# Chunked attention and an ELU feed-forward layer in fp32: unit 0's weights loaded ahead of v, nine element-wise operations moved to GpSimd, a new order of the head

## The chip, the cores and the metric

One core of a Trainium2 chip runs the whole program. The metric is the time of one execution in microseconds, as the device reports it; the number given is the median of three runs. Lower is better.

## The reference

```python
def _attn_ref(q, k, v):                 # (8, 8, 576, 64) each, float32
    # chunks of 64 tokens: q_c, k_c, v_c
    scores = scale * np.matmul(q_c, k_c.transpose(0, 1, 2, 4, 3))
    scores = scores - np.max(scores, axis=-1, keepdims=True)
    attn = np.exp(scores)
    attn = attn / (np.sum(attn, axis=-1, keepdims=True) + 1e-09)
    return np.matmul(attn, v_c).reshape(B, H, S, D)

def _moe_ref(x, w_in, w_out):           # x (4608, 512), w_in (512, 2048), w_out (2048, 512)
    h = x @ w_in
    g = np.where(h > 0.0, h, alpha * (np.exp(np.minimum(h, 0.0)) - 1.0))
    return g @ w_out
# x is the attention's output with the heads put side by side: (batch * seq, heads * head_dim)
```

## The kernel before

**Tiles and blocks.** The 4608 tokens are cut into 36 tiles of 128 tokens (two chunks of 64), four tiles to a block of 512, nine blocks. A tile's attention for all eight heads gives 128 rows of x; a block's four tiles give x of 512 tokens, on which the feed-forward layer works: 16 products H0 to H15 (a slice of 128 hidden units each, `hidden`, 12 matmuls of 128x512), each followed by the elu and by a second product O0 to O15 that adds to four accumulators (`second`, 12 matmuls).

**Words of two parts.** The layer's products run in a reduced fp32 format with high and low words: x = xhi + xlo, w = hi + lo, g = ghi + glo, and each product is the sum of three (high by high, high by low, low by high). So every weight slice has to be prepared once. A unit u is the input weights of slice u and the output weights of slice u - 1 (unit 0 has input weights alone). `load_unit` loads it from memory (L118, L125) into one of three buffers; the weights lie there in another format, and `prepare_units` (ScalarE, L139 and L144) and `merge_units` (VectorE: a clamp L161, two merges L168 and L172; then ScalarE casts the high words, L179) make fp32 of them. `subtract_next` makes the low words: lo = w - hi (L185, one instruction for wi_lo, one for wo_lo).

**The head.** `early_attention` makes the first tiles. Its steps: TensorE transposes q and k (L270), ScalarE copies them (L277), TensorE makes the scores (L248), VectorE takes the largest and subtracts it (L283, L299), ScalarE takes the exponential (L303), VectorE sums, adds, inverts and multiplies (L305 to L308, the last being the product of the probabilities with 1 / z), TensorE turns the probabilities (L315), ScalarE copies them (L322), TensorE multiplies by v (L256), and the result goes to xhi on ScalarE (L425) and xlo on VectorE (L426), or is kept for a later block (L420). For tiles 2, 4 and 5 (`BY_HEAD`) the exponential runs as eight instructions with their sums (L293), and VectorE has no sum to make.

**The order.** The engines' orders are written by hand, as strings of items that the program reads one after another; an item issues one step, and each engine runs its instructions in the order in which they were issued. `START` holds the four tiles of block 0 and first units: `q0`, `k0`, `v0` are loads of a tile on SP's queue, `u0` the load of a unit, a digit the next step of that tile, `r` the next step of ScalarE on a unit, `d` the next of VectorE, `s` a subtraction. `FIRST_BLOCK` holds block 0's layer with the attention of tiles 4 to 7 and the other units: `H` a first product, `e` the next of four steps of an elu (relu and exponential on ScalarE, L468 and L469; elu step on VectorE, L471; ghi on ScalarE, L476; glo on VectorE, L479), after whose last the second product waits to be issued, `P` that second product, `L4` the loads of tile 4. SP's queue issues the loads in the order of the items as well. GpSimd does nothing here until it forms sums of weights from about 120 us on (`combine`, L510). Later blocks (`SECOND_BLOCK` and on) follow with other strings.

Of the kernel before, what the change touches and what calls it, by code (L numbers as in the profile page):

```python
# [10 lines left out]
F32 = mybir.dt.float32  # L11
# [9 lines left out]
def kernel(  # L21
# [19 lines left out]
    nc = tc.nc  # L41
# [138 lines left out]
                merged.append((parts[i], w))  # L180
            yield

    def subtract_next():
        (hi, lo), w = merged.pop(0)
        nc.vector.tensor_tensor(out=lo, in0=w, in1=hi.bitcast(F32), op=ALU.subtract)  # L185

    preparation = prepare_units()
    merged = []
# [72 lines left out]
    def first_halves(pair_of_banks):  # L261
        return pair_of_banks[:, :, :NK * C].rearrange("p i (h t) -> p i h t", h=NK)

    def early_attention(tt: int, q_sb, k_sb, get_v, kT, at, a_pool, get_banks, put, by_head: bool):


        both = get_banks()
        for i, src in enumerate((q_sb, k_sb)):
            for hp in range(NK):
                nc.tensor.transpose(  # L270
                    out=both[:, i, hp * P:(hp + 1) * P], in_=src[:, 2 * hp:2 * hp + 2, :],
                    identity=ident,
                )
# [12 lines left out]
        z = sm.tile([P, 2, NK, 1], F32, name="z")
        if by_head:

            nc.vector.tensor_scalar_mul(mx, mx, -SCALE)
            yield  # L290
            for j in range(2):
                for h in range(NK):
                    nc.scalar.activation(  # L293
                        out=a_heads[:, j, h, :], in_=scores[:, j, h, :], func=AF.Exp, scale=SCALE,
                        bias=mx[:, j, h, :], accum_out=z[:, j, h, :],
                    )
            yield
        else:
            nc.vector.tensor_tensor(  # L299
                out=a_heads, in0=scores, in1=mx.broadcast_to([P, 2, NK, C]), op=ALU.subtract  # L300
            )
            yield
            nc.scalar.activation(out=a, in_=a, func=AF.Exp, scale=SCALE)  # L303
            yield
            nc.vector.tensor_reduce(out=z, in_=a_heads, axis=AX.X, op=ALU.add)  # L305
        nc.vector.tensor_scalar_add(z, z, 1e-9)
        nc.vector.reciprocal(z, z)
        nc.vector.tensor_tensor(  # L308
            out=a_heads, in0=a_heads, in1=z.broadcast_to([P, 2, NK, C]), op=ALU.mult
        )  # L310
# [129 lines left out]
    def hidden(f: int):  # L440
        hi, lo = w_in_slices(f)
        h = ps_h.tile([P, TB], F32, name="h")
        if f:
            for kt in range(NK):
                three(h, hi[:, kt, :], lo[:, kt, :], xhi[:, kt, :], xlo[:, kt, :],
                      kt == 0, kt == NK - 1)
        else:
            terms = [(w, xhi, kt) for w in (hi, lo) for kt in range(NK)]
            terms += [(hi, xlo, kt) for kt in range(NK)]
            for i, (w, x, kt) in enumerate(terms):  # L450
                nc.tensor.matmul(h, lhsT=w[:, kt, :], rhs=x[:, kt, :], start=i == 0,  # L451
                                 stop=i == len(terms) - 1)
        return h
# [564 lines left out]
    def warm(n: int):  # L1018
# [5 lines left out]

    BY_HEAD = (2, 4, 5)
    START = (
        "q0 k0 q1 k1 w13 v0 0 1 0 q2 0 k2 q3 0 k3 1 1 v1 0 2 v2 1 3 0 2 2 v3 1 2 3 u0 3 1 2 u1 0 "
        "r r 1 3 1 0 3 2 2 d u2 d 1 0 r d 3 3 2 s 2 0 r d 1 d 3 r 2 3 3"  # L1030
    )
    FIRST_BLOCK = (
# [7 lines left out]
    )  # L1040
    SECOND_BLOCK = (
# [83 lines left out]
    w0 = ctx.enter_context(tc.tile_pool(name="w0", bufs=1))  # L1125
    weights.append((*w_in_tiles(w0), *w_out_tiles(w0)))
    with (
        tc.tile_pool(name="start", bufs=NTT) as start,
        tc.tile_pool(name="ps_start", bufs=NTT, space=bass.MemoryType.PSUM) as ps_start,
    ):  # L1130
# [6 lines left out]
        def start_step(item: str):  # L1137
            tt = int(item)
            if tt not in tiles:
                tiles[tt] = early_attention(  # L1140
                    tt, *[loaded[kind, tt] for kind in "qk"], lambda: loaded["v", tt],
                    start.tile([P, NK, P], F32, name="kT"), start, start,
                    lambda: start_banks() if tt else warmed[0],
                    split_first_x, tt in BY_HEAD)
            next(tiles[tt])

        for item in START.split():
# [5 lines left out]
            elif kind in "qkv":  # L1153
                loaded[kind, int(n)] = load_heads(
                    {"q": q, "k": k, "v": v}[kind], f"{kind}_sb", int(n) * P, start)
            elif kind == "r":
                next(preparation)
            elif kind == "d":
                next(merging)
            elif kind == "s":  # L1160
                subtract_next()
            else:
                start_step(item)

# [48 lines left out]
    for item in FIRST_BLOCK.split():  # L1213
# [12 lines left out]
            next(early_tiles[item])  # L1226
        elif item == "d":
            next(merging)
        elif item == "s":
            subtract_next()  # L1230
        elif item == "r":
            next(preparation)
        elif item[0] == "u":
# [711 lines left out]
```

## Time and profile before

| | |
|---|---|
| time, median of 3 runs | 825.24 us (823.83 to 828.67) |
| the profiled execution's own time | 825.15 us |
| its span | 823.4 us |
| TensorE busy | 804.4 us (98% of the span) |
| VectorE busy | 613.1 us (74%) |
| ScalarE busy | 523.5 us (64%) |
| GpSimd busy | 171.1 us (21%) |
| granted clock of TensorE over the span | 0.999 of full speed |

The span is the time from the first to the last instruction of the program in the profile; the execution's time has 1.75 us around it. Busy shares are means over stages that differ: the head, in which the first tiles pass from engine to engine, and the long rest, in which matmuls follow each other. PE in the profile is TensorE, PEld its weight loads, DVE VectorE, ACT ScalarE, POOL GpSimd; L315 is line 315 of the kernel before.

### The profile page before, as it was taken

The numbers are of one execution on the slowest core, as the hardware profiler recorded it, in microseconds if no ns is written. First come the engines' busy times: TensorE is split into PE (matmuls) and PEld (weight loads), VectorE is DVE, ScalarE is ACT, GpSimd is POOL, SyncE is SP. The second block draws the span as 40 slices with busy tenths as digits, with TensorE's granted clock in tenths as the row PEclk, the third lists the DMA queues.
The fourth block names the chain that finished last, engine by engine and source line by source line (L and its number), as shares of the span: only waits on it lengthen the run. The fifth ranks groups of instructions, "written<-read, shape, count | busy, mean of one in ns | idle before, by whom it ended". The sixth has DMA issues, their size and how long they took to land.

```text
span 823.4 us, 15851 instructions
## 1 busy us (share of the span) xinstructions
PE 804.4 (98%) x5853; PEld 655.6 (80%) x5853; DVE 613.1 (74%) x914; ACT 523.5 (64%) x990; POOL 171.1 (21%) x149
## 2 busy tenths in 40 slices
PE   6799999999999999999999999999999999999997
PEld 5688878888778878878888888778788888888885
DVE  4999997666776659767656867868889956557964
ACT  5999885544554546766666445888867737776451
POOL 0000014264525531443111254000020100000100
PEclk9999999999999999999999999999999999999999
DMA  9976994889778887689986789999876585566755
GB/s 234 272 212 209 270 328 130 244 243 267 219 215 231 231 269 205 202 241 281 283 235 188 218 246 299 286 322 287 249 204 206 195 269 193 193 196 190 226 186 149
DMA packets 183229, 191.90 MB, mean 233 GB/s; under 512 B 84720, under 2 KB 151792, under 8 KB 183152
## 3 DMA queue, kind: packets, MB, share of 16 engines
q1 hardware_dynamic: 182512, 188.80, 77.2%
q0 software_dynamic: 640, 2.10, 0.6%
q8 instruction: 46, 0.75, 0.4%
q14 instruction: 31, 0.25, 0.1%
HBM read 144.18 MB, written 42.99 MB: 227 GB/s over the span
## 4 chain that ended last, share of the span: by engine, by line
PE 83%; DMA 8%; SPq 3%; ACT 2%; DVE 2%; issue 1%; DVEq 0%; ACTq 0%
PE o L434 43%; PE h L434 34%; DMA ring<-a_dram 3%; PE ps_a L248 2%; PE ps_a L256 2%; SPq L206 2%; PE h L451 1%; DMA st<-in_moe_w_out_dram 1%; DMA kept<-in_k_dram 1%; DMA a_dram<-wi_lo 1%; DMA kept<-in_q_dram 1%; DMA a_dram<-wi_hi 1%; DMA v_sb<-in_v_dram 1%; PE ps_a L315 1%; DMA ring<-w_dram 1%
## 5 line engine op out<-in xcount | busy, mean ns | idle before, releaser
L434 PE MATMUL o<-wo_hi,ghi 128*128 128x512 f32 x272 | 107.6, 396 | 0.0
L434 PE MATMUL o<-wo_hi,glo 128*128 128x512 f32 x272 | 106.1, 390 | 0.3 <-DVE glo L479 0.3
L434 PE MATMUL o<-wo_lo,ghi 128*128 128x512 f32 x272 | 106.0, 390 | 0.0
L434 PE MATMUL h<-xhi,wi_hi 128*128 128x512 f32 x228 | 84.0, 397 | 0.1
L434 PE MATMUL h<-xlo,wi_hi 128*128 128x512 f32 x228 | 82.3, 390 | 0.0
L434 PE MATMUL h<-xhi,wi_lo 128*128 128x512 f32 x180 | 70.3, 390 | 0.0
L434 PEld LDWEIGHTS o<-wo_hi,glo 128*128 128x128 f32 x272 | 51.1, 188 | 11.7 <-DVE glo L479 0.7
L434 PEld LDWEIGHTS o<-wo_hi,ghi 128*128 128x128 f32 x272 | 51.0, 188 | 11.1
L434 PEld LDWEIGHTS o<-wo_lo,ghi 128*128 128x128 f32 x272 | 51.1, 188 | 10.2
L510 POOL TENSOR_TENSOR kept<-wi_hi,wi_lo 128x512 f32<-128x512 f32 x16 | 21.7, 1376 | 158.8 <-DVE xf L172 118.2
L471 DVE SCALAR_TENSOR_TENSOR e<-e,h 128x512 f32<-128x512 f32 x48 | 32.8, 684 | 25.2 <-ACT e L469 24.8
L434 PE MATMUL o<-split,ring 128*128 128x512 f32 x216 | 51.0, 390 | 0.0
L434 PEld LDWEIGHTS h<-xhi,wi_hi 128*128 128x128 f32 x228 | 42.6, 188 | 9.8 <-ACT kept L785 0.8
L434 PEld LDWEIGHTS h<-xlo,wi_hi 128*128 128x128 f32 x228 | 42.8, 188 | 8.5
L434 PEld LDWEIGHTS o<-split,ring 128*128 128x128 f32 x216 | 40.5, 188 | 8.4
L393 ACT COPY unturned<-turned 128x512 f32<-128x512 f32 x28 | 17.4, 621 | 46.0 <-DVE turned L388 37.9
L468 ACT ACTIVATE e<-h 128x512 f32<-128x512 f32 x48 | 28.6, 596 | 25.0 <-PE h L434 22.5
L476 ACT CAST ghi<-e 128x512 fp32r<-128x512 f32 x48 | 29.8, 621 | 19.8 <-DVE e L471 19.6
L746 POOL TENSOR_TENSOR glo<-e,ghi 128x512 fp32r<-128x512 f32 x16 | 20.7, 1296 | 96.9 <-ACT ghi L744 96.9
L434 PE MATMUL h<-split,ring 128*128 128x512 f32 x168 | 40.3, 391 | 0.0
L1492 ACT ACTIVATE e<-e 128x512 f32<-128x512 f32 x64 | 39.5, 630 | 1.0
L434 PEld LDWEIGHTS h<-xhi,wi_lo 128*128 128x128 f32 x180 | 33.8, 188 | 7.5 <-DVE wi_lo L185 0.4
(225 smaller groups left out, 2011.3 us busy)
## 6 DMA issues: line engine op xcount, KB each, us to landing
ring<-a_dram SPq DMA_DIRECT2D x56, 512.0 KB, 5.3
ring<-w_dram SPq DMA_DIRECT2D x56, 512.0 KB, 4.3
wi_hi<-a_dram SPq DMA_DIRECT2D x56, 256.0 KB, 5.3
kept<-in_q_dram SPq DMA_DIRECT2D x100, 128.0 KB, 3.8
kept<-in_k_dram SPq DMA_DIRECT2D x100, 128.0 KB, 4.0
wo_lo<-lo_dram SPq DMA_DIRECT2D x20, 512.0 KB, 5.8
v_sb<-in_v_dram SPq DMA_DIRECT2D x32, 256.0 KB, 5.4
st<-in_moe_w_in_dram SPq DMA_DIRECT2D x16, 512.0 KB, 4.9
```

The costliest lines, as they stand in the source:

```text
L206: nc.sync.dma_start(out=dst[p0:p0 + n], in_=src[b, :, s0:s0 + n, :].rearrange("h s d -> s h d"))
L248: nc.tensor.matmul(scores[halves[c], j, hp, :], lhsT=qT[halves[j], hp, halves[c]], rhs=kT[halves[j], hp, halves[c]], start=True, stop=True,)
L256: nc.tensor.matmul(x_ps[halves[j], c, hp, :], lhsT=v_sb[halves[c], 2 * hp + j, :], rhs=aT[halves[c], :, j * NK + hp], start=True, stop=True,)
L315: nc.tensor.matmul(turned_ps[half, h, :], lhsT=a[half, h, :], rhs=ident[half, half], start=True, stop=True,)
L393: nc.scalar.copy(out=unturned, in_=turned)
L434: nc.tensor.matmul(ps, lhsT=a, rhs=b, start=start, stop=stop, skip_group_check=onto)
L468: nc.scalar.activation(out=e, in_=h, func=AF.Relu, scale=-1.0)
L471: nc.vector.scalar_tensor_tensor(out=e, in0=e, scalar=-1.0, in1=h, op0=ALU.add, op1=ALU.max)
L476: nc.scalar.copy(out=ghi, in_=e)
L510: nc.gpsimd.tensor_tensor(out=out, in0=a, in1=b, op=op)
L746: engine.tensor_tensor(out=lo, in0=e, in1=hi.bitcast(F32), op=ALU.subtract)
L1492: nc.scalar.activation(out=units[u], in_=units[u], func=AF.Exp, scale=-1.0)
```

## The change

Four parts. Lines below L183 move by one, those of the layer by one or two, so that L308 before is L309 now, L471 is L472.

1. On SP's queue the first unit's load stands ahead of the v of the first tiles, the second unit's between v0 and v1; q3 and k3 change places. Tile 4's loads stand ahead of unit 3's.
2. `early_attention` gets an argument: for tiles 1 and 2 the product of the probabilities with 1 / z runs on GpSimd. The block of the head schedules GpSimd by hand as well.
3. A second kind of subtraction item, `S`, runs on GpSimd; seven of `FIRST_BLOCK`'s are of that kind.
4. `START` and the first third of `FIRST_BLOCK` have a new order. For H1 and H2 the twelve matmuls come, as for H0, as three groups of four, now with the low words of w last.

```diff
-    def subtract_next():
+    def subtract_next(engine=nc.vector):
         (hi, lo), w = merged.pop(0)
-        nc.vector.tensor_tensor(out=lo, in0=w, in1=hi.bitcast(F32), op=ALU.subtract)
+        engine.tensor_tensor(out=lo, in0=w, in1=hi.bitcast(F32), op=ALU.subtract)
...
-        nc.vector.tensor_tensor(
+        (nc.gpsimd if normal_on_pool else nc.vector).tensor_tensor(
             out=a_heads, in0=a_heads, in1=z.broadcast_to([P, 2, NK, C]), op=ALU.mult
         )
...
-        if f:
+        if f > 2:
             for kt in range(NK):
                 three(h, hi[:, kt, :], lo[:, kt, :], xhi[:, kt, :], xlo[:, kt, :],
                       kt == 0, kt == NK - 1)
         else:
-            terms = [(w, xhi, kt) for w in (hi, lo) for kt in range(NK)]
-            terms += [(hi, xlo, kt) for kt in range(NK)]
+            terms = [(hi, x, kt) for x in (xhi, xlo) for kt in range(NK)]
+            terms += [(lo, xhi, kt) for kt in range(NK)]
...
+    ENGINE_OF = {"s": nc.vector, "S": nc.gpsimd}
...
-        "q0 k0 q1 k1 w13 v0 0 1 0 q2 0 k2 q3 0 k3 1 1 v1 0 2 v2 1 3 0 2 2 v3 1 2 3 u0 3 1 2 u1 0 "
+        "q0 k0 q1 k1 w13 0 1 q2 0 0 k2 0 k3 q3 u0 v0 u1 v1 v2 v3 1 2 1 1 0 0 2 1 2 r r 1 d 3 2 "
...
-        "H r u3 r d L4 d e s 4 d 4 e e s r d e u4 H d s 4 e s r P e 4 d e e H 4 e d 4 L5 e s u5 d P "
+        "H d L4 r e d s 4 r u3 r 4 d e d e u4 S r d e H d 4 s s e P e 4 r e e H d P 4 e d e s "
...
+        tc.manual_schedule(engines={mybir.EngineType.Pool}),
...
-                    split_first_x, tt in BY_HEAD)
+                    split_first_x, tt in BY_HEAD, tt in (1, 2))
...
-            elif kind == "s":
-                subtract_next()
+            elif kind in "sS":
+                subtract_next(ENGINE_OF[kind])
```

**The loads.** SP's queue from tile 1's k on, before. `st` is the buffer of a unit's weights, `q_sb`, `k_sb`, `v_sb` those of a tile.

```order
L206 DMA k_sb<-in_k_dram 128x8x64
L206 DMA v_sb<-in_v_dram 128x8x64
L206 DMA q_sb<-in_q_dram 128x8x64
L206 DMA k_sb<-in_k_dram 128x8x64
L206 DMA q_sb<-in_q_dram 128x8x64
L206 DMA k_sb<-in_k_dram 128x8x64
L206 DMA v_sb<-in_v_dram 128x8x64 x3
L118 DMA st<-in_moe_w_in_dram 128x4x256 x2
L125 DMA st<-in_moe_w_out_dram 128x1024
```

And now, from the load behind tile 1's k on:

```order
L206 DMA q_sb<-in_q_dram 128x8x64
L206 DMA k_sb<-in_k_dram 128x8x64 x2
L206 DMA q_sb<-in_q_dram 128x8x64
L118 DMA st<-in_moe_w_in_dram 128x4x256
L206 DMA v_sb<-in_v_dram 128x8x64
L118 DMA st<-in_moe_w_in_dram 128x4x256
L125 DMA st<-in_moe_w_out_dram 128x1024
L206 DMA v_sb<-in_v_dram 128x8x64 x3
```

Unit 0's weights were the thirteenth load and are the ninth; unit 1's stood behind them and now stand between v0 and v1.

**ScalarE between the last tile of block 0 and the scores of tile 4, before.** `xhi` are the casts that H0 needs, L468 and L469 the relu and exponential of H0, L139 and L144 the two steps on a unit, L179 the casts of a unit's high words.

```order
L425 CAST xhi<-ps_a 128x2x4x64
L322 COPY qT<-ps_a 128x512
L139 ACTIVATE st<-st 128x1024
L425 CAST xhi<-ps_a 128x2x4x64 x2
L144 ACTIVATE st<-st 128x1024
L139 ACTIVATE st<-st 128x1024
L179 CAST wi_hi<-xf 128x512
L179 CAST wo_hi<-xf 128x4x4x32
L468 ACTIVATE e<-h 128x512
L469 ACTIVATE e<-e 128x512
L277 COPY qT<-ps_a 128x512
```

And now (L469 and L470 are the relu and the exponential of H0):

```order
L426 CAST xhi<-ps_a 128x2x4x64 x3
L139 ACTIVATE st<-st 128x1024
L144 ACTIVATE st<-st 128x1024
L139 ACTIVATE st<-st 128x1024
L469 ACTIVATE e<-h 128x512
L470 ACTIVATE e<-e 128x512
L179 CAST wi_hi<-xf 128x512
L179 CAST wo_hi<-xf 128x4x4x32
L144 ACTIVATE st<-st 128x1024
L139 ACTIVATE st<-st 128x1024
L278 COPY qT<-ps_a 128x512
```

The three casts to xhi stand together. Unit 1's first step, which stood ahead of them, stands behind them; the casts of unit 1, unit 2's second step and unit 3's first, which stood ahead of H0's relu, stand behind its exponential.

**VectorE ahead of H3, before.** The three rows on z and a are tile 4's; L471 is the elu step of H2.

```order
L172 SCALAR_TENSOR_TENSOR xf<-st,xf 128x1024
L306 TENSOR_SCALAR z<-z 128x8
L307 RECIPROCAL z<-z 128x8
L308 TENSOR_TENSOR a<-a,z 128x512
L471 SCALAR_TENSOR_TENSOR e<-e,h 128x512
L185 TENSOR_TENSOR wi_lo<-xf,wi_hi 128x512
```

And now, from the load behind tile 1's k on:

```order
L172 SCALAR_TENSOR_TENSOR xf<-st,xf 128x1024
L472 SCALAR_TENSOR_TENSOR e<-e,h 128x512
L185 TENSOR_TENSOR wi_lo<-xf,wi_hi 128x512
L307 TENSOR_SCALAR z<-z 128x8
L308 RECIPROCAL z<-z 128x8
L309 TENSOR_TENSOR a<-a,z 128x512
```

Tile 4's three steps moved from ahead of the elu step of H2 to behind it and behind a subtraction.

## Rows read from the trace of the kernel before

**Rows 1.** The line of the page on the engines' busy time, its share of the span and the number of instructions.

```profile
PE 804.4 (98%) x5853; PEld 655.6 (80%) x5853; DVE 613.1 (74%) x914; ACT 523.5 (64%) x990; POOL 171.1 (21%) x149
```

**Rows 2.** The table of stretches: the stretch in us, its length, then for TensorE (PE), its weight loads, VectorE, ScalarE and GpSimd the busy us (and instructions), granted clock of TensorE, share of the DMA engines, GB/s.

```profile
0.00:29.00 29.00, 17.75 (x430) 15.32 (x431) 16.94 (x33) 18.71 (x43) 0.70 (x6) 1.00 0.92 251
29.00:200.00 171.00, 171.00 (x1303) 138.47 (x1304) 143.28 (x196) 123.02 (x216) 38.38 (x37) 1.00 0.80 240
```

**Rows 3.** The list of TensorE's waits over the whole run: who waited, for whom, us in total, times, longest.

```profile
PE ps_a L315 <- DVE a L308: 3.6, 3, 1.6
PE ps_a L270 <- DMA k_sb<-in_k_dram: 2.2, 3, 1.6
```

**Rows 4.** Timeline of TensorE: start in us, us, line, operation, out<-in, shapes, count, and in brackets the idle time before and what ended it. The transposes of k of tile 2 and of q and k of tile 3 (L270), the first matmul of H0 (L451), of H1, tile 4's turn (L315) and the first matmul of H3 (L434).

```profile
10.29 0.66 PE L270 MATMUL ps_a<-ident,k_sb 128*128 128x128 f32 x4 [0.16 <-DMA k_sb<-in_k_dram]
11.24 0.66 PE L270 MATMUL ps_a<-ident,q_sb 128*128 128x128 f32 x4 [0.29 <-DMA q_sb<-in_q_dram]
13.52 0.66 PE L270 MATMUL ps_a<-ident,k_sb 128*128 128x128 f32 x4 [1.63 <-DMA k_sb<-in_k_dram]
...
28.89 1.20 PE L451 MATMUL h<-xhi,wi_hi 128*128 128x512 f32 x4 [1.34 <-ACT xhi L425]
...
32.53 0.48 PE L434 MATMUL h<-xhi,wi_hi 128*128 128x512 f32 x1
...
44.46 1.15 PE L315 MATMUL ps_a<-ident,a 64*64 64x64 f32 x32
45.53 0.50 PE L434 MATMUL h<-xhi,wi_hi 128*128 128x512 f32 x1
```

**Rows 5.** Timeline of ScalarE, the same columns. The first of tile 2's eight exponentials and the read of the last one's sum (L293), unit 0's two steps (L139, L144), two copies (L322), steps of units 2 and 3 (L144, L139), the casts of unit 1 (L179), the relu of H0 (L468); then the relu and the exponential of H2 (L468, L469) and the cast wo_hi behind them (L179).

```profile
15.93 0.31 ACT L293 ACTIVATE a<-ps_a,mx 128x64 f32<-128x64 f32 x1 [0.65 <-DVE mx L289]
...
18.16 0.24 ACT L293 ACTIVATION_READ_ACCUMULATOR a<-ps_a,mx 128x1 f32 x1
18.63 0.67 ACT L139 ACTIVATE st<-st 128x512 f32<-128x512 f32 x1 [0.23 <-DMA st<-in_moe_w_in_dram]
19.19 0.65 ACT L144 ACTIVATE st<-st 128x512 uint32<-128x512 uint16 x1
19.75 1.04 ACT L322 COPY qT<-ps_a 128x512 f32<-128x512 f32 x2
...
28.71 1.17 ACT L144 ACTIVATE st<-st 128x1024 uint32<-128x1024 uint16 x1
29.74 1.17 ACT L139 ACTIVATE st<-st 128x1024 f32<-128x1024 f32 x1
30.83 0.62 ACT L179 CAST wi_hi<-xf 128x512 fp32r<-128x512 f32 x1
31.36 0.61 ACT L179 CAST wo_hi<-xf 128x512 fp32r<-128x512 f32 x1
32.00 0.60 ACT L468 ACTIVATE e<-h 128x512 f32<-128x512 f32 x1
...
42.01 0.63 ACT L468 ACTIVATE e<-h 128x512 f32<-128x512 f32 x1
42.67 0.63 ACT L469 ACTIVATE e<-e 128x512 f32<-128x512 f32 x1
...
43.72 0.61 ACT L179 CAST wo_hi<-xf 128x512 fp32r<-128x512 f32 x1
```

**Rows 6.** Timeline of VectorE, the same columns. Tile 2's first small step on z (L306) and its product of probabilities (L308), unit 0's last merge (L172), the same of unit 1 (L172), a clamp (L161); then tile 4's product (L308), the elu step of H2 (L471) and a wi_lo subtraction (L185).

```profile
18.84 0.16 DVE L306 TENSOR_SCALAR z<-z 128x8 f32<-128x8 f32 x1
...
19.27 0.69 DVE L308 TENSOR_TENSOR a<-a,z 128x512 f32<-128x512 f32 x1
...
21.13 0.70 DVE L172 SCALAR_TENSOR_TENSOR xf<-st,xf 128x512 uint32<-128x512 uint32 x1
...
29.59 1.22 DVE L172 SCALAR_TENSOR_TENSOR xf<-st,xf 128x1024 uint32<-128x1024 uint32 x1
30.72 0.69 DVE L161 TENSOR_SCALAR st<-st 128x1024 f32<-128x1024 f32 x1
...
42.80 0.69 DVE L308 TENSOR_TENSOR a<-a,z 128x512 f32<-128x512 f32 x1
43.41 0.68 DVE L471 SCALAR_TENSOR_TENSOR e<-e,h 128x512 f32<-128x512 f32 x1
44.01 0.68 DVE L185 TENSOR_TENSOR wi_lo<-xf,wi_hi 128x512 fp32r<-128x512 f32 x1
```

**Rows 7.** GpSimd: of the table of groups the subtraction glo = e - ghi (count, busy us, mean ns, idle before); then the timeline of VectorE around 120 us and of GpSimd there; last, a 128x256 instruction of GpSimd at 134 us.

```profile
L479 POOL TENSOR_TENSOR glo<-e,ghi 128x512 fp32r<-128x512 f32 x13 | 16.8, 1292 | 33.4 <-ACT ghi L476 33.4
...
119.31 0.68 DVE L471 SCALAR_TENSOR_TENSOR e<-e,h 128x512 f32<-128x512 f32 x1
120.09 1.29 DVE L185 TENSOR_TENSOR wi_lo<-xf,wi_hi 128x512 fp32r<-128x512 f32 x1
121.31 1.22 DVE L479 TENSOR_TENSOR glo<-e,ghi 128x512 fp32r<-128x512 f32 x1
...
119.54 1.30 POOL L510 TENSOR_TENSOR kept<-wi_hi,wi_lo 128x512 f32<-128x512 f32 x1 [118.23 <-DVE xf L172]
120.91 1.06 POOL L510 TENSOR_TENSOR kept<-kept 128x256 f32<-128x256 f32 x1
...
133.94 0.74 POOL L510 TENSOR_TENSOR kept<-kept 128x256 f32<-128x256 f32 x1
```

More of the change, by code (lines that the diff above doesn't have):

```diff
@@ L262, in first_halves, with early_attention @@
         return pair_of_banks[:, :, :NK * C].rearrange("p i (h t) -> p i h t", h=NK)
-    def early_attention(tt: int, q_sb, k_sb, get_v, kT, at, a_pool, get_banks, put, by_head: bool):
+    def early_attention(tt: int, q_sb, k_sb, get_v, kT, at, a_pool, get_banks, put, by_head: bool,
+                        normal_on_pool: bool = False):
         both = get_banks()
@@ L1023, in warm @@
             nc.tensor.transpose(out=warm_ps[:, i % 4, :], in_=ident, identity=ident)
+    ENGINE_OF = {"s": nc.vector, "S": nc.gpsimd}
     BY_HEAD = (2, 4, 5)
     START = (
-        "q0 k0 q1 k1 w13 v0 0 1 0 q2 0 k2 q3 0 k3 1 1 v1 0 2 v2 1 3 0 2 2 v3 1 2 3 u0 3 1 2 u1 0 "
-        "r r 1 3 1 0 3 2 2 d u2 d 1 0 r d 3 3 2 s 2 0 r d 1 d 3 r 2 3 3"
+        "q0 k0 q1 k1 w13 0 1 q2 0 0 k2 0 k3 q3 u0 v0 u1 v1 v2 v3 1 2 1 1 0 0 2 1 2 r r 1 d 3 2 "
+        "3 0 3 d 0 1 2 3 2 1 1 3 d 3 0 2 s 0 3 2 2 3 2 1 3 3 r r d u2"
     )
     FIRST_BLOCK = (
[7 rows of a table removed]
[8 rows of a table added]
     )
@@ L1228 @@
             next(merging)
-        elif item == "s":
-            subtract_next()
+        elif item in ENGINE_OF:
+            subtract_next(ENGINE_OF[item])
         elif item == "r":
```

13 rows, old and new, of the table FIRST_BLOCK are left out of this document.

## The prediction

> **What bounds the kernel now.** The busy line of the page says TensorE: 804.4 of 823.4 us [rows 1]. The table of stretches then says where the other 19 us lie: in the first 29 us TensorE is busy for 17.75 us, and from 29 to 200 us for 171.00 of 171.00 [rows 2]. So a change to the head can give back what lies ahead of the first product of the first layer (H0, at 28.89) [rows 4], and everything that reaches TensorE later than it does now, up to 200 us, is paid in full: there is no idle time to absorb it. The list of TensorE's waits names the two largest: 3.6 us for VectorE's normalized probabilities and 2.2 us for k [rows 3].
>
> The last number to keep is 45.53, the start of the fourth hidden product (H3) [rows 4]. I follow the change from the loads to H3 and compare there, since up to H3 the two orders differ most and after it TensorE has no gap in either direction to lose. The profiled execution took 825.15 us, 0.09 below the median of 825.24, so the sum is made against 825.15.
>
> **The loads.** Unit 0's input weights now stand directly behind q3, ninth on SP's queue, v0 and unit 1 behind them. SP issues the same DMAs in all, and q and k arrive one place earlier. q3 has landed by 11.24; it came 0.95 after k2, and k3 then 2.28 after q3, which is 1.33 more than that spacing [rows 4]. Unit 0 is 512 KB, two such loads: it lands at 13.1 (11.24 + 2 x 0.95) or, if it meets that extra 1.33, at 14.5. I take the middle, 13.8, and keep both ends. ScalarE meets it early: behind its wait stand the copies of q and k of tile 3, tile 0's copy and tile 2's exponentials.
>
> **H0.** From 13.8 on ScalarE runs the unit's two steps (18.63 to 19.75, 1.12), three copies at 0.5, and eight exponentials (15.93 to 18.40, 2.47) [rows 5]: 18.9. VectorE's two small steps on z take 0.43 (18.84 to 19.27) [rows 6]: 19.35. Then tile 2's product, now on GpSimd, at 1.29 by the nearest kind of row [rows 7] where VectorE took 0.69: 20.65. Next to it VectorE goes straight from the reciprocal to unit 0's merge (L172, 0.70) [rows 6], which reads two SBUF tensors. What that does is seen 100 us later: while GpSimd works (119.54 to 120.84), VectorE's wi_lo subtraction, with two SBUF inputs, takes 1.29, the glo one behind it 1.22 beside the next GpSimd instruction, and GpSimd's own 128x256 there takes 1.06 where another takes 0.74; the elu step ahead of them, with one input in PSUM, stays at 0.68 [rows 7]. So two such instructions on the two engines do not overlap: who comes second waits. GpSimd comes second here and loses 0.65: 21.3. The other end is 0, if it starts first.
>
> TensorE then turns tiles 2 and 3 (44.46 to 45.53, 1.07 each) [rows 4]: 23.45. Copy 0.5, tile 2's product with v 0.7 meanwhile, three xhi casts at 0.5 on ScalarE from 24.2: H0 starts at 25.8, **3.1 us earlier** than 28.89. With unit 0 at 13.1 and no collision it would be 24.5, with 14.5, 26.5. Tile 1's product on GpSimd costs nothing: TensorE is waiting then for the copies behind the unit's two steps.
>
> **From H0 to H3.** The price is on ScalarE. Before, units 1 and 2 and the first step of unit 3 were done by the relu of H0, most of it in waits of the head; now unit 1 begins only behind the casts to xhi. ScalarE has to do L139, L144, L139 (1.09 + 1.03 + 1.09 = 3.2) from 25.7 on [rows 5], so relu of H0 starts at 28.9, just as H0 ends (32.00 - 28.89 = 3.1 after its start before). From that relu to the relu of H2 took 10.01 us (32.00 to 42.01) without a gap [rows 5]. The new order has four more instructions in between: cast wi_hi 0.53, cast wo_hi 0.64, L144 1.03, L139 1.09, in all 3.3 [rows 5]. The cast wi_hi also waits 0.3 for VectorE's two merges of 1.22 [rows 6] behind unit 1's L144 (27.9 + 2.45 = 30.35 against 30.1). Relu of H2: 28.9 + 10.0 + 3.3 + 0.3 = 42.5, against 42.01. **Of the 3.1 us nothing is left, 0.5 is owed.**
>
> Then comes what is new on VectorE: tile 4's z and product stood ahead of the elu step of H2 (42.80, then 43.41) and needed nothing of it [rows 6]; now they stand behind it. TensorE's turn of tile 4 stands ahead of H3 in both orders. So: 42.5 + exp 0.66 + 0.63 [rows 5], elu step and wi_lo 0.6 each [rows 6], z 0.43: 45.4. There the product would take 0.7; but the cast wo_hi ends 2.32 after the relu (42.01 to 44.33) [rows 5] and releases GpSimd's second subtraction at 44.8, which runs to 46.1 or, held 0.2 by wi_lo, 46.3. The product has two SBUF inputs and waits: 46.8. Turn 1.07: H3 at 47.9, **2.4 us late** (1.7 without that hold).
>
> **After H3.** Five more subtractions run on GpSimd. VectorE is relieved of 0.6 each, which buys nothing where TensorE has no wait. Each can hold a VectorE instruction of two SBUF inputs for up to 0.6 (1.29 - 0.69). Bounds: 0, and 5 x 0.6 = 3.0 if every hold reaches TensorE. I take 0.4, one of them in part, since the consumers of wo_lo come some 5 us later and only a product of probabilities stands directly ahead of TensorE. The term order of H1 and H2 (xhi with w_hi, xlo with w_hi, then w_lo) lets w_lo come later; its twelve matmuls are the same. H1 waits on TensorE for the cast wi_hi, until about 31 (32.53 before) [rows 4]; that wait costs nothing of its own, since ScalarE, not H2, is what the relu of H2 waits for. POOL's place in the hand-made order adds no instruction.
>
> **Sum:** -3.1 + 5.5 + 0.4 = +2.8, so 825.15 + 2.8 = **828.0 us**. 0.5% is about what a measurement of this kernel can tell from no change: 821.1 to 829.4 counts as the same.
>
> **Rivals.**
> (a) The lead is kept: 825.15 - 3.1 = 822.0, not slower. This needs the relu of H2 by about 39.5, so that the turn of tile 4 is ready when the second layer's second product ends. For it: TensorE shows no wait in 29 to 200 [rows 2], and VectorE is relieved. Against it: ScalarE's row without a gap, 32.00 to 42.01, and the 3.3 us now inside it [rows 5]. It decides if those four instructions find gaps. Chance 0.12.
> (b) The two engines do not hold each other here: -0.65 at H0, -0.7 at H3 and -0.4 after, 826.2. For it: the elu step is not stretched; against it: both subtractions are [rows 7]. Chance 0.15.
> (c) VectorE's clamp L161 is held as well. It does 1024 columns in 0.69 where the merges take 1.22, twice the rate [rows 6, 7], and reads one SBUF tensor; no row before has it beside GpSimd. In the new order it stands behind wi_lo of unit 1, just when the first GpSimd subtraction runs, and would lose up to 1.2, of which 0.5 reaches H3 through the cast wi_hi that waits for the merges; one more such meeting after H3 costs 1.0. 828.0 + 1.5 = 829.5. [...] Chance 0.25.
> (d) The forecast, 0.48. That the change does not do what it says, unit 0 landing at 18.6 as before [rows 5], would add 4.8; its place in the queue excludes that.
>
> **The numbers.** The likeliest is 828.0. The range 822.5 to 830.5 leaves out most of (a) and the cases above (c) with a late unit 0, together under 2 in 10. Faster by over 0.5% needs (a) with unit 0 at 13.1 besides: 0.03. Slower by over 0.5%: half of (c), and the forecast with several holds reaching TensorE: 0.2. The rest, 0.77, is within 0.5%.
>
> **What would show it.** Right: H0 near 25.8; ScalarE without a gap from the xhi casts to the relu of H2 near 42.5; TensorE waiting some 2 to 3 us for VectorE's L309 ahead of H3 near 47.9; GpSimd's second product and VectorE's L309 stretched beyond 1.29 and 0.69. Wrong: H3 before 45.5, or a head in which H0 is not earlier than 28, or TensorE waiting over 1 us in all between H3 and 200. If L161 takes 1.9 instead of 0.69 beside GpSimd, (c) holds.

## The result and the profile after

The changed kernel takes 831.41 us (median of 22 runs, 827.71 to 836.84) where the kernel before took 825.93 beside it (22 runs): ratio 1.0066, 95% interval 1.0052 to 1.0081, so **5.5 us slower** (4.3 to 6.7). The forecast was +2.8. The profiled execution took 830.03 us, 4.88 more than that of before.

The table of stretches for the kernel after (columns as in [rows 2]):

```profile
0.00:29.00 29.00, 21.25 (x449) 17.72 (x449) 16.84 (x32) 19.46 (x44) 3.06 (x8) 1.00 0.96 256
29.00:200.00 171.00, 164.67 (x1267) 132.51 (x1268) 142.75 (x184) 120.92 (x212) 48.10 (x41) 1.00 0.77 234
```

TensorE gains 3.5 us in the head, and then stands idle for 6.3 us in a stretch in which it had not waited once [rows 2]. TensorE's rows after, at the places of [rows 4] (start, us, engine, line, operation, in brackets the idle time ahead and what ended it):

```profile
25.07 1.20 PE L452 MATMUL h<-xhi,wi_hi 128*128 128x512 f32 x4 [0.77 <-ACT xhi L426]
30.34 1.20 PE L452 MATMUL h<-xhi,wi_hi 128*128 128x512 f32 x4 [1.35 <-ACT wi_hi L179]
36.39 0.50 PE L435 MATMUL o<-wo_hi,glo 128*128 128x512 f32 x1 [1.12 <-DVE glo L480]
38.80 1.07 PE L452 MATMUL h<-xhi,wi_hi 128*128 128x512 f32 x4
46.91 1.15 PE L316 MATMUL ps_a<-ident,a 64*64 64x64 f32 x32 [2.51 <-ACT st L139]
47.99 0.50 PE L435 MATMUL h<-xhi,wi_hi 128*128 128x512 f32 x1
...
65.54 0.50 PE L435 MATMUL o<-wo_hi,glo 128*128 128x512 f32 x1 [0.19 <-DVE glo L480]
71.31 1.15 PE L316 MATMUL ps_a<-ident,a 64*64 64x64 f32 x32 [0.49 <-DVE a L309]
...
75.24 0.39 PE L435 MATMUL h<-xhi,wi_hi 128*128 128x512 f32 x1
```

The last row is the first matmul of H7. In the kernel before it is this one:

```profile
71.34 0.39 PE L434 MATMUL h<-xhi,wi_hi 128*128 128x512 f32 x1
```

H0 comes 3.82 earlier (25.07), H1 2.19, H2 0.12, and H3 2.46 later (47.99). The wait of 2.51 ahead of H3 is put down to ScalarE; it is VectorE's product (L309), which ends at 46.76. Behind H3 the lateness grows at three more places, by 0.42, 0.46 and 0.56, to 3.90 at H7 (75.24 where it was 71.34); it then keeps between 3.5 and 4.1 up to 275 us.

ScalarE, with the relus of H0 and H2 and the two casts of wi_hi between them (compare [rows 5]):

```profile
28.21 0.60 ACT L469 ACTIVATE e<-h 128x512 f32<-128x512 f32 x1
29.67 0.62 ACT L179 CAST wi_hi<-xf 128x512 fp32r<-128x512 f32 x1 [0.20 <-DVE xf L172]
35.77 0.62 ACT L179 CAST wi_hi<-xf 128x512 fp32r<-128x512 f32 x1 [0.34 <-DVE xf L172]
42.01 0.64 ACT L469 ACTIVATE e<-h 128x512 f32<-128x512 f32 x1
```

The relu of H0 starts 3.79 earlier than in [rows 5], the relu of H2 at 42.01 as before to the hundredth: ScalarE spends the whole lead. Now VectorE and GpSimd beside each other (compare [rows 6, 7]):

```profile
19.72 0.69 DVE L306 TENSOR_REDUCE z<-a 128x8 f32<-128x512 f32 x1
...
30.32 0.69 DVE L185 TENSOR_TENSOR wi_lo<-xf,wi_hi 128x512 fp32r<-128x512 f32 x1 [0.68 <-ACT wi_hi L179]
30.93 1.81 DVE L161 TENSOR_SCALAR st<-st 128x1024 f32<-128x1024 f32 x1
...
43.95 0.68 DVE L185 TENSOR_TENSOR wi_lo<-xf,wi_hi 128x512 fp32r<-128x512 f32 x1
44.56 1.25 DVE L307 TENSOR_SCALAR z<-z 128x8 f32<-128x8 f32 x1
46.07 0.69 DVE L309 TENSOR_TENSOR a<-a,z 128x512 f32<-128x512 f32 x1
...
53.74 2.13 DVE L168 SCALAR_TENSOR_TENSOR xf<-st 128x1024 uint32<-128x1024 uint32 x1
55.91 2.21 DVE L172 SCALAR_TENSOR_TENSOR xf<-st,xf 128x1024 uint32<-128x1024 uint32 x1
58.04 0.68 DVE L480 TENSOR_TENSOR glo<-e,ghi 128x512 fp32r<-128x512 f32 x1
...
59.41 1.81 DVE L161 TENSOR_SCALAR st<-st 128x1024 f32<-128x1024 f32 x1
...
64.80 0.68 DVE L480 TENSOR_TENSOR glo<-e,ghi 128x512 fp32r<-128x512 f32 x1
...
68.33 1.73 DVE L172 SCALAR_TENSOR_TENSOR xf<-st,xf 128x1024 uint32<-128x1024 uint32 x1
...
70.47 0.69 DVE L309 TENSOR_TENSOR a<-a,z 128x512 f32<-128x512 f32 x1
```

```profile
14.86 1.05 POOL L309 TENSOR_TENSOR a<-a,z 128x512 f32<-128x512 f32 x1 [13.55 <-DVE z L308]
19.27 1.31 POOL L309 TENSOR_TENSOR a<-a,z 128x512 f32<-128x512 f32 x1 [3.36 <-ACT qT L323]
30.89 1.30 POOL L185 TENSOR_TENSOR wo_lo<-xf,wo_hi 128x512 fp32r<-128x512 f32 x1 [10.31 <-ACT wo_hi L179]
44.42 1.35 POOL L185 TENSOR_TENSOR wo_lo<-xf,wo_hi 128x512 fp32r<-128x512 f32 x1 [12.23 <-ACT wo_hi L179]
53.38 1.41 POOL L185 TENSOR_TENSOR wi_lo<-xf,wi_hi 128x512 fp32r<-128x512 f32 x1 [7.60 <-ACT wi_hi L179]
54.76 2.28 POOL L185 TENSOR_TENSOR wo_lo<-xf,wo_hi 128x512 fp32r<-128x512 f32 x1
59.37 1.30 POOL L185 TENSOR_TENSOR wo_lo<-xf,wo_hi 128x512 fp32r<-128x512 f32 x1 [2.33 <-ACT wo_hi L179]
...
66.60 2.37 POOL L185 TENSOR_TENSOR wo_lo<-xf,wo_hi 128x512 fp32r<-128x512 f32 x1
```

In these rows a held instruction shows no idle time ahead of it; it shows as a longer one (the clamp at 30.93 takes 1.81, where 0.69 before [rows 6]). Read the rows from 53.38 to 58.12 as a chain: GpSimd's wi_lo ends at 54.79; VectorE's L168, issued at 53.74, ends 1.08 after that (55.87); GpSimd's wo_lo, issued at 54.76, ends 1.17 after that (57.04); VectorE's L172, issued at 55.91, ends 1.08 after that (58.12). They take turns: each of the three ends 1.08 to 1.17 behind the end of the other engine's instruction, nearly all that it takes elsewhere in this execution (1.22 and 1.23 for the two merges at 47.89 and 49.14, 1.30 for the wo_lo at 59.37). Not every VectorE instruction is held: the sum of L306, with one SBUF input, takes 0.69 at 19.72, all of it beside GpSimd's product (19.27 to 20.58).

### The profile page after: what moved, and what is told of

The parts are those of the page before. It is cut to its first block, busy times and chain, and to the rows that moved or that the text cites. A ratio compares the mean times of both kernels' runs of the same rounds, so it can differ in the third digit from the quotient of the medians.

```text
span 828.2 us, 15862 instructions
## 1 busy us (share of the span) xinstructions
PE 805.7 (97%) x5853; PEld 655.2 (79%) x5853; DVE 614.2 (74%) x905; ACT 524.2 (63%) x990; POOL 186.0 (22%) x158
## 4 chain that ended last, share of the span: by engine, by line
PE 80%; DMA 7%; DVE 5%; ACT 4%; SPq 2%; issue 1%; POOL 0%; DVEq 0%; ACTq 0%; POOLq 0%
PE o L435 43%; PE h L435 30%; DMA ring<-a_dram 3%; PE h L452 2%; PE ps_a L248 2%; PE ps_a L256 2%; DMA kept<-in_q_dram 2%; DVE xf L172 1%; DMA wi_hi<-a_dram 1%; DVE xf L168 1%; SPq L206 1%; PE ps_a L316 1%; DMA st<-in_moe_w_in_dram 1%; DMA v_sb<-in_v_dram 1%; DVE st L161 1%
## 5 line engine op out<-in xcount | busy, mean ns | idle before, releaser
L435 PE MATMUL h<-xhi,wi_hi 128*128 128x512 f32 x204 | 74.3, 396 | 0.1
L435 PE MATMUL h<-xlo,wi_hi 128*128 128x512 f32 x204 | 73.0, 389 | 0.0
L435 PE MATMUL h<-xhi,wi_lo 128*128 128x512 f32 x156 | 60.8, 390 | 0.0
L472 DVE SCALAR_TENSOR_TENSOR e<-e,h 128x512 f32<-128x512 f32 x48 | 32.8, 683 | 26.7 <-ACT e L470 26.5
L469 ACT ACTIVATE e<-h 128x512 f32<-128x512 f32 x48 | 28.7, 598 | 26.0 <-PE h L435 22.6
L435 PEld LDWEIGHTS h<-xhi,wi_hi 128*128 128x128 f32 x204 | 38.1, 188 | 8.9 <-ACT kept L786 0.8
L435 PEld LDWEIGHTS h<-xlo,wi_hi 128*128 128x128 f32 x204 | 38.3, 188 | 7.7
L435 PEld LDWEIGHTS h<-split,ring 128*128 128x128 f32 x168 | 31.2, 188 | 7.0 <-DMA ring<-w_dram 0.4
```

The costliest lines, as they stand in the source:

```text
L435: nc.tensor.matmul(ps, lhsT=a, rhs=b, start=start, stop=stop, skip_group_check=onto)
L469: nc.scalar.activation(out=e, in_=h, func=AF.Relu, scale=-1.0)
L472: nc.vector.scalar_tensor_tensor(out=e, in0=e, scalar=-1.0, in1=h, op0=ALU.add, op1=ALU.max)
```

## The experiments

All times beside the kernel before on the same chip. The us given in the text are worked out from the ratio; where the medians say something else, both stand. H0, H3 and H7 are read from one profiled execution each, as us later (+) or earlier (-) than 28.89, 45.53 and 71.34. A star marks a number behind a place in that execution's head where the granted clock fell for a few us, to 0.50 to 0.57 of full speed in the lowest stretch of 2 us (more on that under chance, below).

| kernel | median, us | ratio to before (95%) | H0 | H3 | H7 |
|---|---|---|---|---|---|
| the change | 831.41 | 1.0066 (1.0052 to 1.0081) | -3.82 | +2.46 | +3.90 |
| e1 all nine on VectorE | 828.15 | 1.0025 (1.0009 to 1.0041) | -2.27* | +2.47* | +2.53* |
| e2 subtractions on VectorE | 828.18 | 1.0034 (1.0011 to 1.0057) | -4.54 | +0.19 | +0.23 |
| e3 products on VectorE | 831.74 | 1.0072 (1.0058 to 1.0086) | -2.99 | +3.55* | +6.88* |
| e4 tile 4's product first | 828.56 | 1.0032 (1.0013 to 1.0051) | -3.53* | +0.13* | +2.26* |
| e5 mended | 826.67 | 1.0025 (1.0003 to 1.0046) | -2.19* | +0.55* | +0.85* |
| e6 reordered | 825.89 | 1.0022 (1.0001 to 1.0042) | -3.20 | -0.13 | +0.28 |
| e7 old order, subtractions on GpSimd | 825.92 | 1.0011 (0.9993 to 1.0029) | -0.17* | +0.16* | +1.58* |
| e8 before, TensorE late | 830.33 | 1.0081 (1.0051 to 1.0111) | +4.76* | +4.76* | +4.76* |
| e9 before with the new head | 826.73 | 1.0016 (0.9998 to 1.0035) | -3.06 | -0.16 | -0.16 |
| e10 before again | 826.77 (1 run) | | -1.18 | +0.45* | +0.45* |
| e11 change again | 830.56 (1 run) | | -4.16 | +3.33* | +5.36* |
| e12 e2 and e4 together | 826.55 | 0.9999 (0.9980 to 1.0018) | -3.47 | -0.05 | +0.54 |

**e1, e2, e3: which of the nine.** The order of the change is kept; operations go back to VectorE.

```diff
# e1 and e2
-    ENGINE_OF = {"s": nc.vector, "S": nc.gpsimd}
+    ENGINE_OF = {"s": nc.vector, "S": nc.vector}
# e1 and e3
-                    split_first_x, tt in BY_HEAD, tt in (1, 2))
+                    split_first_x, tt in BY_HEAD, False)
```

> The changed kernel with its order kept to the letter, but all nine moved operations (seven subtractions, two products) back on VectorE. Theory 1 (GpSimd's element-wise work holds VectorE): the clamp L161 at 30.9 us takes 0.69 instead of 1.81, the small z step L307 ahead of tile 4's product 0.17 instead of 1.25. The cast wi_hi at 35.77 then waits 0.34 less and the product comes 1.08 earlier: H3 at 47.99 - 1.4 = 46.6, that is 1.0 later than in the kernel before, and the merges at 53 to 69 us take 1.2 each, so the 1.4 us that the changed kernel loses between 58 and 72 us are gone: +1.0 at 72 us instead of +3.9. Whole kernel: +1.0 against before, at most +2.6 if the 1.6 us that the changed kernel lost behind 205 us come with any late head. Theory 2 (the order alone does it): H3 stays near 48.0, +3.5 to 3.9 at 72 us, whole kernel +5.5 as the change itself.

> The changed kernel with the seven subtractions back on VectorE, the two products of tiles 1 and 2 still on GpSimd. Theory 1 (holds): it is the subtractions that hold, so H3 near 46.5 and the whole kernel +0.8 to +1.0 against before (+2.4 if the loss behind 205 us comes along), as with all nine back. Theory 2 (order alone): +5.5. Theory 3 (the products of tiles 1 and 2 carry a good part of the loss): at least 1 us above the kernel with all nine on VectorE.

> The changed kernel with the two products of tiles 1 and 2 back on VectorE, the seven subtractions still on GpSimd. Theory 1 (the subtractions hold): H0 at 25.1 to 25.5 (VectorE does 0.6 more ahead of tile 3's product, TensorE turns tile 2 some 0.5 earlier), the rest shifted as before: H3 48.0 to 48.2, +3.9 at 72 us, whole kernel +5.5 to +5.7. Theory 3 (the products): H0 over 0.5 earlier than 25.07 and the whole kernel at least 1 us faster than the changed one.

VectorE in e2, where the subtractions are back:

```profile
30.18 0.69 DVE L161 TENSOR_SCALAR st<-st 128x1024 f32<-128x1024 f32 x1
...
43.37 0.17 DVE L307 TENSOR_SCALAR z<-z 128x8 f32<-128x8 f32 x1
43.81 0.69 DVE L309 TENSOR_TENSOR a<-a,z 128x512 f32<-128x512 f32 x1
```

and TensorE in e2:

```profile
44.65 1.15 PE L316 MATMUL ps_a<-ident,a 64*64 64x64 f32 x32 [1.66 <-DVE a L309]
45.72 0.50 PE L435 MATMUL h<-xhi,wi_hi 128*128 128x512 f32 x1
```

Without the subtractions on GpSimd the clamp is back at 0.69 and the z step at 0.17, H3 is near its old place, and nothing is lost behind it (+0.19 at H3, +0.23 at H7). Some of that is luck: unit 0's first step on ScalarE starts at 12.69 here and at 13.64 in the change, and H0 is 0.72 earlier than there; an estimate with the change's H0 is some +0.9 at H3. The whole kernel is at +2.8 us (0.9 to 4.7; +1.5 by the medians) in place of +5.5, above what was expected; e1 agrees with +2.1 (+1.5 by the medians), though its H3 does not: its clock fell at 20 to 24 us (to 0.60 and 0.55 in two stretches of 2 us). e3 is the change over again: the two products cost nothing that can be measured. What is left in e2 is the wait of 1.66 for tile 4's product.

**e4 and e12: the place of tile 4's product.** In `FIRST_BLOCK`, the item that issues it moves ahead of the elu step of H2; e12 has the edit of e2 besides.

```diff
-  ... 4 r e e H d P 4 e d e s u5 4 d e L5 ...
+  ... 4 r e e H d P 4 e d 4 e s u5 d e L5 ...
```

> The changed kernel with one item moved: tile 4's z steps and product stand ahead of the elu step of H2 again, as in the kernel before; GpSimd keeps its nine operations. The step of the prediction that was right (H3 2.4 us late since the product stands behind the elu step and is held): z at 42.7, product until 43.9, TensorE free from O1 at 44.2, turn 1.07: H3 at 45.3 to 45.5, within 0.2 of before. Behind it the holds of the merges stay: +1.3 at 72 us, whole kernel +1.3 (up to +2.9 if the loss behind 205 us comes along). Rival: the relu of H2 and the chain on ScalarE set H3, not the product: H3 stays above 47 and the whole kernel above +4.5.

> The changed kernel with two edits: its seven subtractions back on VectorE, and tile 4's z steps and product ahead of the elu step of H2; all else as in the change, ScalarE's steps too. With the first edit alone H2 came 1.54 earlier than before and H3 0.19 later, behind a wait of 1.66 for that product. Theory 1 (that place is what ate the rest of the lead): in an execution whose granted clock doesn't fall in the head, H3 1.2 to 1.6 earlier than before, the same at 72 us, whole kernel -1.5 to +0.5 (what a median can show of it). Rival (ScalarE's row and the units' arrival set H3 whatever the product does, as in the mended and the reordered kernel): H3 within 0.5 of before, whole kernel +0.5 to +2.

e4: H3 within 0.13 of before and the whole at +2.6 (1.1 to 4.2; +1.9 by the medians), as expected; the loss behind H3 is still there, 2.13 by H7 where 1.3 was expected. e12: ratio 0.9999, no difference from before. TensorE and ScalarE in e12:

```profile
44.41 1.15 PE L316 MATMUL ps_a<-ident,a 64*64 64x64 f32 x32 [0.30 <-ACT wi_hi L179]
45.49 0.50 PE L435 MATMUL h<-xhi,wi_hi 128*128 128x512 f32 x1
```

```profile
32.70 1.17 ACT L139 ACTIVATE st<-st 128x1024 f32<-128x1024 f32 x1 [0.45 <-DMA st<-in_moe_w_out_dram]
```

The wait of 1.66 is 0.30, but H3 stands where it stood before, not 1.2 to 1.6 earlier: there the rival was right, and on the whole kernel theory 1.

**Two edits together take the loss away.** The subtractions back: from +5.5 to +2.8. The product first: from +5.5 to +2.6. Both: -0.1 (-1.7 to +1.5), with the loads, the head, the two products on GpSimd and the order of terms of the change kept. How the loss divides between the two is not shown. The ratios give 2.7 and 2.8, each uncertain by some 2 us; the medians give 4.0 and 3.6; and at H7, where the change is 3.90 late, e2 is at +0.23, e4 at +2.26 and e12 at +0.54, so that in the traces of the head the subtractions alone are most of it. Nor is it sure that nothing is left: e5 and e6 below hold both edits too and come out at +2.1 and +1.8, in intervals that overlap with that of e12.

**e9: the new head alone.** The kernel before with the change's `START`; one item each of `r` and `d`, which the new head leaves undone, stand at the front of its own `FIRST_BLOCK`.

```diff
-  START       "q0 k0 q1 k1 w13 v0 0 1 0 q2 0 k2 q3 0 k3 1 1 v1 ... u0 3 1 2 u1 0 ..."
+  START       "q0 k0 q1 k1 w13 0 1 q2 0 0 k2 0 k3 q3 u0 v0 u1 v1 v2 v3 ..."
-  FIRST_BLOCK "H r u3 r d L4 d e s ..."
+  FIRST_BLOCK "r d H r u3 r d L4 d e s ..."
```

> The kernel before with the new order of the loads and of the head alone (unit 0 ahead of v), its own order behind H0 (with one step on ScalarE and one merge, that the new head leaves undone, put ahead of it), its own order of the terms and no element-wise work on GpSimd. Theory 1 (what comes early at H0 is spent before H3, on ScalarE's steps and on units 1 to 3 that land no earlier; the loss is made behind it): H0 2.5 to 4.5 earlier, H3 within 0.8 of 45.53, the same at 72 us, whole kernel between -0.8 and +1.5. Rival (the early unit 0 is worth its lead, and only the new order behind H0 spoils it): H3 2.5 or more earlier and the whole kernel at -2.5 or below.

Theory 1 held. H0 comes 3.06 earlier, H3 0.16, the whole kernel is the same (1.0016, 0.9998 to 1.0035). ScalarE's relus of H0 and H2 in e9:

```profile
31.94 0.58 ACT L468 ACTIVATE e<-h 128x512 f32<-128x512 f32 x1
...
41.99 0.64 ACT L468 ACTIVATE e<-h 128x512 f32<-128x512 f32 x1
```

They stand where they stood in [rows 5] (32.00 and 42.01): the steps of the units that ScalarE used to do while it waited for H0 now stand between H0 and its relu. The early load is worth nothing by itself.

**e5 and e6: can the lead be kept?** e5 is e12 with one of unit 1's two steps on ScalarE moved ahead; e6 moves some 15 items more.

```diff
# e5, START
-  ... 2 1 1 3 d 3 0 2 s 0 3 2 2 3 2 1 3 3 r r d u2
+  ... 2 1 1 3 d r 3 0 2 s 0 3 2 2 3 2 1 3 3 r d u2
# e6, the front of FIRST_BLOCK (START's tile steps are shuffled as well)
-  H d L4 r e d s 4 r u3 r 4 d e d e u4 S r d e H ...
+  H d L4 r r e d d e s 4 u3 r 4 e u4 d S r d e H ...
```

> The changed kernel with three things mended: the seven subtractions back on VectorE, tile 4's product ahead of the elu step of H2, and one of unit 1's two steps on ScalarE moved into the gap of 0.86 us that ScalarE has at 21.0 us (the products of tiles 1 and 2 stay on GpSimd). With the subtractions on VectorE alone H3 came at 45.72, 0.19 later than in the kernel before, behind a wait of 1.66 for tile 4's product: that wait goes, and 0.5 more through the step on ScalarE. H3 at 43.5 to 44.1, and the lead stays to 200 us: -1.4 to -2.0 there. Theory 1 (holds, place of the product, ScalarE's row): whole kernel -2.0 to 0 against before, the upper end if the stages behind 200 us give 1 to 2 us away as in the profiled executions so far. Rival: something else of the new order eats the lead, and the kernel stays at +1.5 or above.

> As the mended kernel, with some 15 items more moved in the head: VectorE's merge steps of unit 0 and tiles' steps swapped in places, two of ScalarE's steps of unit 2 and its own place among the elu steps of H0, so that TensorE waits less for glo of O0 (1.1 us in the changed kernel) and for the cast of unit 1's w_in (1.3). Estimate from these waits: H3 at 42.1 to 42.6, 2.9 to 3.4 earlier than before, carried to 200 us; whole kernel -3.2 to -1.0, the fastest of all so far. Rival: the time of the head does not reach the end, since the stages behind 200 us wait for DMA: whole kernel within 0.5 of the mended one.

Both miss what was expected, and are not faster than before: e5 is at +2.1 (0.2 to 3.8; +1.2 by the medians) and e6 at +1.8 (0.1 to 3.5; +0.4 by the medians). In e6, whose clock stayed up, H3 comes 0.13 earlier, not 2.9 to 3.4. ScalarE in e6:

```profile
32.63 1.16 ACT L139 ACTIVATE st<-st 128x1024 f32<-128x1024 f32 x1 [1.50 <-DMA st<-in_moe_w_out_dram]
```

Unit 3's output weights land at 32.6 there (29.2 before): in the new order their load stands behind those of tile 4 and is issued at 27.5 (22.3 before), and the DMA engines are busy for 0.90 of the first 29 us (0.92 before [rows 2]). So in e6, where other loads were pulled ahead in that stretch, unit 3's output weights came 3.4 us later. As far as these rows show, ScalarE's row and the arrival of the units set H3; neither e6 nor any other kernel here beats the kernel before.

**e7: the subtractions on GpSimd in the old order.** The seven subtractions with the same numbers in the sequence become `S` in the `FIRST_BLOCK` of before, and GpSimd is scheduled by hand as in the change; nothing else changes.

```diff
-  "H r u3 r d L4 d e s 4 d 4 e e s r d ... 4 d 4 s H r e ... e e s r d u7 d s e d P ..."
+  "H r u3 r d L4 d e s 4 d 4 e e S r d ... 4 d 4 S H r e ... e e S r d u7 d S e d P ..."
```

> The kernel before with one thing of the change alone: the same seven subtractions (by their number in the sequence) run on GpSimd, at the places in the order of the kernel before; loads, products and order are those of before. Theory 1 (holds cost in any order): H0 as before, H3 +0.2, and between H3 and O6 about what the changed kernel lost there (1.4), up to 2.2 if tile 5's product is held by a whole subtraction: +1 to +2.5 at 72 us, whole kernel +1 to +2.5. Rival (the holds hurt only because the new order left VectorE late): within 0.5 of before.

+0.16 at H3 and +1.58 at H7, behind O5 (which the expectation calls O6), as expected; by the whole kernel (+0.9, -0.6 to +2.4) the two theories can't be told apart.

**e8, e10, e11: what happens behind 200 us.** The profiled execution after loses another 2.0 us between 200 and 700 us, where its program is that of before. e8 only starts H0 late (`w42` at the end of `START`); e10 and e11 are the two kernels again.

> The kernel before with 42 more transposes of the identity on TensorE, at the very end of the head, whose result nobody reads: the same order and engines, only H0 starts later, by about 3.6 (42 at 0.125, the pitch of the 128x128 transposes at 12.3 us, from the last product with v at 27.5). It asks what a late head alone does to the rest. Theory A (a late head is carried 1:1): the same shift at H3, at 72, at 200 us and at the end; whole kernel up by that shift, within 0.7. Theory B (a later head also loses at the DMA waits behind 200 us, as the changed kernel's profile shows 2.0 more there): the whole kernel up by the shift and 1.0 to 2.0 more.

> The kernel before itself, for a second profile. Between 200 and 600 us the profiled executions of eight kernels of the same program there lost 0.2 to 3.6 us against the one of before, and one gained 0.6. Theory A (chance: the first profiled execution of before met few DMA waits there): the second one loses 0.5 to 2 against the first between 200 and 700 us, at the waits for the ring and for the turned tiles. Theory B (the loss belongs to the change): the second one is within 0.3 of the first at every product there.

> The changed kernel itself, for a second profile. Theory 1 (the holds are of the program, not of the execution): L161 near 31 us over 1.6, L307 ahead of tile 4's product over 1.0, H3 2.2 to 2.8 late against before and another 1.0 to 1.8 by 72 us. Theory A (chance behind 200 us): the loss from 200 to 700 us differs from the 2.0 of the first profile by over 0.5; theory B (it belongs to the change): 1.7 to 2.3 again.

TensorE in 480 to 600 us, in the order before, after, e10 (before again), e11 (the change again):

```profile
480.00:600.00 120.00, 118.50 (x808) 95.59 (x807) 92.03 (x138) 90.19 (x216) 19.94 (x15) 1.00 0.95 287
```

```profile
480.00:600.00 120.00, 118.04 (x805) 94.84 (x804) 90.42 (x133) 90.19 (x210) 23.02 (x17) 1.00 0.96 281
```

```profile
480.00:600.00 120.00, 117.25 (x805) 95.01 (x804) 92.28 (x137) 89.85 (x213) 21.32 (x15) 1.00 0.97 284
```

```profile
480.00:600.00 120.00, 118.01 (x808) 95.56 (x807) 90.56 (x133) 90.80 (x214) 23.00 (x17) 1.00 0.97 283
```

The kernel before itself stands idle there for 1.5 us in one execution and 2.75 in another, 1.96 and 1.99 in the changed one. From 200 to 700 us e10 loses 2.2 against the first execution of before, e11 0.8, the first of the change 2.0: chance. e8's shift of 4.76 at H0 (3.6 expected) is 4.76 at H7, 4.5 at 184 us and 5.5 at the end; the medians say 4.87, the ratio 6.7 (4.2 to 9.2). Theory A fits, but that interval does not exclude B. In e11 the holds are there again: the clamp at 1.80, the z step at 1.25, the two merges at 2.13 and 2.21. Behind H3 it loses 2.03 by H7, more than in the first execution and than the 1.0 to 1.8 expected; its H3 stands behind a fall of the clock (0.57 from 36 to 40 us).

The clock is chance of the same kind. In the head of e10:

```profile
26.00:28.00 2.00, 0.63 (x25) 0.49 (x18) 1.76 (x3) 2.00 (x4) 0.00 (x0) 1.00 1.21 267
28.00:30.00 2.00, 2.00 (x7) 1.52 (x7) 2.00 (x3) 2.00 (x3) 0.00 (x0) 0.57 0.74 162
30.00:32.00 2.00, 2.00 (x7) 1.57 (x6) 1.92 (x3) 0.80 (x2) 0.00 (x0) 0.58 0.59 149
```

The granted clock (third number from the end) falls to 0.57 and 0.58 of full speed in the two stretches from 28 to 32 us, after one in which TensorE was busy for 0.63 of 2 us; H0 takes 4.44 us there (27.71 to 32.15) instead of 2.86 (28.89 to 31.75). In 8 of the 14 profiled executions it fell so once within the first 60 us, at places from 14 to 52 us, in the kernels of the old order as in those of the new, to 0.50 to 0.57 in the lowest 2 us; in those of before and of the change that the text compares it did not.

## Why the prediction was wrong

**Right, up to H3.** Unit 0's first step on ScalarE started at 13.64, behind a wait of 1.07 for its weights (forecast 13.8). H0 came at 25.07 (25.8): the forecast hold of 0.65 on tile 2's product was 0.26 (1.31 against 1.05 for tile 1's), since VectorE's merge had begun at 19.04 and ended at 19.68, 0.41 behind the start of GpSimd's product (19.27). From the relu of H0 to the relu of H2 it took 13.80 us (13.6 forecast: 10.0 + 3.3 + 0.3), so the relu of H2 stood at 42.01 (42.5): the lead was eaten on ScalarE, as e9 shows with the head alone. H3 at 47.99 (47.9), 2.46 late (2.4). That it came out so near is luck, since two errors cancel: the relu was 0.5 early, and GpSimd's second subtraction held not the product but the z step of 128x8 ahead of it, to 45.81, which let the reciprocal and the product follow only then (product until 46.76, forecast 46.8).

**Wrong: "After H3", 0.4 us.** This is the step that failed; it measured 1.44 by H7 (2.03 in e11), over the 1 us that the prediction itself named as a sign of being wrong. Its price for one hold, at most 0.6 (1.29 - 0.69), was too low: it was taken from a wi_lo that met the second half of a GpSimd instruction (120.09, beside 119.54 to 120.84 [rows 7]). Here the holds were longer: L161, issued 0.04 behind the start of GpSimd's subtraction, grew by 1.12, the z step, 0.14 behind, by 1.08, and the two merges at 53.74 and 55.91 by 0.91 and 0.99. And "only a product of probabilities stands directly ahead of TensorE" looked at the held instruction and not at the queue behind it. What stands behind a held instruction in VectorE's rows starts within 0.1 us of its end: 32.67 behind 32.74, 45.84 behind 45.81, 61.32 behind 61.22. The two merges held up glo behind them (58.04, behind 58.12), for which TensorE waits at O3: 0.42. The clamp at 59.41 held up the glo of O4 (64.80): 0.46. A merge of 1.73 (68.33) held up tile 5's product (70.47), which was not held itself, ahead of O5: 0.56. The bound of 3.0 for this step did hold, though not by its price: five holds at the measured 1.1 would be 5.5.

**Wrong in weight: rival (c).** The clamp is held, at 1.81 (forecast 1.9). No row of before has the clamp beside GpSimd, so its loss of up to 1.2 was the author's estimate; it came out at 1.12. The z step, a VectorE instruction of eight columns that rival (c) did not name, was held as well, at 1.25 for 0.17. The clamp's price at H3 was 0.34 (the second cast of wi_hi) where 0.5 was said, and its second meeting, at 59.41 us, cost 0.46 of the 1.0 set for it. So the clamp is a third of what was lost behind H3; the other holds are the rest.

**The sum.** By the trace: -3.82 + 6.28 + 1.44 = +3.9 up to H7 against +2.8. So up to H3 the sum was right (+2.5 for +2.4), and the 1.1 that it lacks is the step behind H3. By the whole kernel the loss is 5.5, and by e12 the subtractions and the place of tile 4's product together make it (e5 and e6 leave some 2 us of that in doubt). The trace of the changed kernel shows 3.9 of it in the head. Where the other 1.6 arise stays open: the interval of the 5.5 goes down to 4.3, and the traces of the stages behind 200 us, where before differs from itself by 2.2, can't decide it. The range failed because its upper end took (c) as the worst case and not (c) together with several holds that reach TensorE. Of the 0.9 us by which the time lies above it, 0.7 is no loss: the kernel before took 825.93 beside the change, not 825.24.

## What to carry to other kernels

Before an element-wise operation goes to GpSimd, list what VectorE runs beside it. Here instructions with two SBUF inputs (the merges: 2.13 and 2.21 us for 1.22; wi_lo: 1.29 for 0.68 [rows 6, 7]) and two `tensor_scalar` steps from SBUF to SBUF (the clamp: 1.81 for 0.69; the step on z: 1.25 for 0.17) waited for a GpSimd instruction, up to nearly a whole one, and with them all that was queued behind. Price a meeting at the full GpSimd duration (1.05 to 1.3 us here for 128x512), not at the difference of two durations (0.6 in the forecast, where the holds of the clamp, the z step and the merges at 53.74 and 55.91 cost 0.9 to 1.1). The load that was pulled ahead was worth nothing here, where the engine that works on it (ScalarE) had no free time behind it: in e9 H0 came 3.06 us earlier and H3 0.16. So look for that engine's rows without a gap, and follow the lead to the first place that it must reach.

## What the runs showed of the hardware

The step on z of 128x8, which takes 0.17 us in e2, takes 1.25 beside a GpSimd subtraction (44.56); GpSimd is held as well, its subtraction at 54.76 taking 2.28 where the one at 30.89 takes 1.30. The elu step, which reads PSUM, passes beside GpSimd at 0.68 [rows 7], and so does the sum L306 of 128x512 from SBUF, at 0.69 (19.72). And the granted clock of TensorE fell for some us in the head of 8 of the 14 profiled executions, to 0.50 to 0.57 in the lowest 2 us, by chance: in one of two executions of the kernel before and in one of two of the change. It cost 1.6 us in H0 of e10, where matmuls stand without a gap; in e7 it fell at 14 to 18 us (to 0.50 and 0.69), ahead of waits of the head, and H0 was not late (-0.17).
